# Two first loads on one queue, and four dummy matmuls ahead of the first transpose

## The chip, the cores and the metric

The kernel runs on one core of a Trainium2 chip. A core has five engines that run their own instruction streams and wait for one another through semaphores: TensorE (PE, matmuls and transposes; its weight loads appear as PEld), VectorE (DVE), ScalarE (ACT), GpSimd (POOL) and SyncE (SP). Sixteen DMA engines move data between HBM and the on-chip memory; SP, ACT and POOL issue their transfers. In this kernel POOL's loads run on queue q0 ("software_dynamic"), SP's on q1 and ACT's on q10 (both "hardware_dynamic"); q8 carries instructions.

The metric is the device time of one execution in microseconds (us), here the median of 4 executions: 333.9 us, from 333.14 to 334.2.

## The reference, cut to what matters

Attention with a causal window of 64 positions, over 8 batches and 8 heads of 576 positions with 64 elements each, then a gated feed-forward block on the 4608 x 512 result:

```python
scores = scale * np.matmul(q, k.transpose(0, 1, 3, 2))
mask = (rel >= 0) & (rel < 64)          # rel = query position - key position
attn = softmax(np.where(mask, scores, -1e9))
x = np.matmul(attn, v)                  # -> [4608, 512]
g = x @ w_gate
out = (g / (1 + np.exp(-g)) * (x @ w_val)) @ w_out
```

Inputs and the output are float32. The kernel computes in bfloat16 with float32 accumulation.

## The kernel before, in words

The 4608 tokens are cut into 36 chunks of 128 tokens for the attention and into 9 chunks of 512 tokens for the feed-forward block. For an attention chunk, q and k are transposed (128x128 transposes on PE against an identity matrix, evicted from PSUM by ACT or DVE; for later chunks transposing DMAs on SP), scores are 64-column matmuls, ACT takes their exponential, DVE masks them, PE multiplies by v (which has a column of ones for the sum), DVE divides, and PE transposes the result into xT. The feed-forward block multiplies xT with 128-column blocks of w_gate and w_val (`F`), ACT and DVE form the gated product (`U` is the DVE half), and the last matmuls multiply by w_out (`O`).

The order of the work at the start is written by hand, as two strings of short words in class `_Kernel`: `LOADS`, then `STEPS`. `build` reads them word by word and calls the method that a word names; each call records operations, and `_Graph.emit` later puts every engine's operations in that order into its own stream, with a semaphore wait only where one depends on another engine or on a DMA. The words that matter here:

- `f:0:own` calls `first_load` (L285; the issue has line L291). Chunk 0 is loaded as float32: k into partitions 0 to 63 of the tile ff, q into partitions 64 to 127, 256 KB each. `own` picks the queue of q; k is always on SP:

```python
for eng, p0, src in (("sp", 0, self.k), ("act" if own else "sp", 64, self.q)):
```

- `init` builds the identity, the mask nmask and the zeroed tile wz on DVE (columns 0 to 127 of wz first, at L255; columns 128 to 511 at L271).
- `kq:n`, `v:n`, `w:a:b` issue the loads of chunks and weights on POOL, which casts to bfloat16.
- `warm:65` (L348) puts 65 matmuls of 64 columns on wz at the head of PE's stream. `B:0` (L403) are two matmuls of 512 columns that write the mask into the score banks of chunk 0.
- `ca:0:0` and `cd:0:1` cast the two halves of ff to the bfloat16 tile cc, on ACT (L300) and DVE (L302). Each half holds partitions of both q and k, so both casts need both loads.
- `T:0:1` and `T:0:0` are the first transposes, four a word (L310), each after its half of cc. `ea`, `ed` evict them into kT and qT.
- `W:n` calls `fill` (L359): n matmuls of 512 columns on wz, whose result nobody reads. It looks up the PSUM bank that was free longest and does not reserve it.
- Then chunks 1 to 3: `TQ`, `TK` transposes and `qa`, `kd` evictions, `S` scores (L423), `A0`, `A1` products with v (L473), `M` masks (L439), `N` divisions (L492, L495), `X` transposes (L570), `xa`, `xd` evictions, and from `F:0:7` on the first feed-forward matmuls (L604).

Of the kernel before, what the change touches and what calls it, by code (L numbers as in the profile page):

```python
# [7 lines left out]
B, H, S, D = 8, 8, 576, 64  # L8
DM, DFF = H * D, 1536
T = B * S  # L10
# [139 lines left out]
class _Kernel:  # L150
# [9 lines left out]
    LAST = NFC  # L160
    NI = 1
    LOADS = """
    f:0:1 init kq:1 kq:2 v:0 kq:3 v:1 v:2 v:3 w:7:9 kq:5 kq:4 w:3:4 w:6:7 w:4:5 v:5 w:1:2 v:4 w:9:10 w:2:3 v:6
    w:5:6 v:7 kq:6 w:0:1 kq:7 w:10:12
    """
    STEPS = """
    warm:65 ld:8 wo:0:6 B:0 ca:0:0 cd:0:1 T:0:1 T:0:0 ea:0:1 ed:0:0 TQ:1 qa:1 W:1 S:0 TK:1 ld:9 kd:1 W:1 TQ:2
    qa:2 S:1 B:2 TK:2 kd:2 A0:0 A1:0 M:1 S:2 TQ:3 N:0 B:3 TK:3 qa:3 kd:3 W:1 X:0 A0:1 xa:0 S:3 A1:1 ld:10 A0:2
    N:1 A1:2 ld:11 W:1 A0:3 N:2 A1:3 X:1 xa:1 N:3 W:1 X:2 xa:2 W:3 X:3 F:0:7:0:384 xd:3 U F:0:8 U TK:5 TQ:5
    ka:5 TQ:4 F:0:7:384:512 TK:4 ld:12 qa:4 qd:5 ka:4 U W:2 F:0:3 U S:4 S:5 F:0:6 M:4 F:0:4 M:5 U F:0:1 U U  # L170
    A0:4 A0:5 A1:4 ld:13 wo:6:12 A1:5 F:0:9 N:4 N:5 X:4 F:0:2 U xa:4 X:5 U F:0:5 xd:5 F:1:1:0:128 U TQ:6
    F:1:2:0:256 U TK:6 ld:14 qa:6 F:1:3:0:256 U F:0:0 kd:6 U U S:6 TK:7 TQ:7 F:1:0:0:256 kd:7 F:0:10 M:6 U
    qa:7 U A0:6 S:7 A1:6 ld:15 TQ:8 TK:8 N:6 F:0:11 M:7 ka:8 qd:8 X:6 A0:7 xa:6 U S:8 A1:7 ld:16 F:1:4:0:384
    N:7 F:1:5:0:384 U X:7 U TQ:9 xa:7 F:1:6:0:384 M:8 qa:9 TK:9 U F:1:7 kd:9 TD:10 U A0:8 S:9 A1:8 ld:17 F:1:8
# [610 lines left out]
```

## Time and profile before

| | |
|---|---|
| median of 4 executions | 333.9 us |
| the profiled execution's own time | 334.17 us |
| its span, first to last instruction | 332.4 us |
| PE busy | 325.3 us (98%), 3557 matmuls and 3557 weight loads |
| DVE, ACT, POOL busy | 216.9, 137.4, 115.8 us |
| L310 on cc, the first transposes, start | 6.99 us |
| L604, the first feed-forward matmul, start | 19.31 us |
| L359, dummy matmuls of 512 columns | 10, median 379 ns, longest 631 ns |
| first loads, issue to landing | k on SP 5.7 us, q on ACT 4.1 us |

The profile is of one execution, and its span leaves out what lies before the first and after the last instruction. [...] matmuls that follow one another overlap; what a stream of them costs is read from the distance of their starts. "PEclk" is the clock that TensorE was granted, as a share of its full speed. In a table by windows, each row is a stretch of the span, with every engine's busy time and its number of instructions.

### The profile page before, as it was taken

The numbers are of one execution on the slowest core, as the hardware profiler recorded it, in microseconds if no ns is written. First come the engines' busy times: TensorE is split into PE (matmuls) and PEld (weight loads), VectorE is DVE, ScalarE is ACT, GpSimd is POOL, SyncE is SP. The second block draws the span as 40 slices with busy tenths as digits, with TensorE's granted clock in tenths as the row PEclk, the third lists the DMA queues.
The fourth block names the chain that finished last, engine by engine and source line by source line (L and its number), as shares of the span: only waits on it lengthen the run. The fifth ranks groups of instructions, "written<-read, shape, count | busy, mean of one in ns | idle before, by whom it ended". The sixth has DMA issues, their size and how long they took to land.

```text
span 332.4 us, 8407 instructions
## 1 busy us (share of the span) xinstructions
PE 325.3 (98%) x3557; PEld 166.6 (50%) x3557; DVE 216.9 (65%) x454; ACT 137.4 (41%) x249; POOL 115.8 (35%) x144
## 2 busy tenths in 40 slices
PE   6989999999999999999999999999999999999997
PEld 5654656564454545454545454545454544444444
DVE  6468989994448767676767676767666666555520
ACT  3745456562234525252525243434342522233222
POOL 8999999964008606060706060100000000000000
PEclk9799999999999999999999999999999999999999
DMA  9999999999999999999998989442414111100012
GB/s 132 166 169 172 163 179 156 178 152 150 214 181 114 125 177 76 178 69 187 64 192 61 194 56 182 70 126 34 129 33 127 27 70 28 69 34 32 32 58 103
DMA packets 168837, 38.70 MB, mean 116 GB/s; under 512 B 159328, under 2 KB 164320, under 8 KB 168800
## 3 DMA queue, kind: packets, MB, share of 16 engines
q0 software_dynamic: 122560, 18.62, 81.1%
q1 hardware_dynamic: 45568, 19.21, 28.0%
q8 instruction: 28, 0.46, 0.6%
q10 hardware_dynamic: 672, 0.33, 0.4%
q14 instruction: 9, 0.07, 0.1%
HBM read 37.75 MB, written 9.44 MB: 142 GB/s over the span
## 4 chain that ended last, share of the span: by engine, by line
PE 94%; DVE 2%; DMA 2%; issue 0%; ACT 0%; DVEq 0%
PE ps L604 56%; PE ps L637 28%; PE ps L423 3%; PE ps L536 2%; PE ps L310 2%; DMA ff<-in_k_dram 2%; DVE xb L495 1%; PE ps L473 1%; PE ps L667 1%; PE ps L570 1%; PE ps L403 0%; DVE rc L492 0%; PE ps L359 0%; DVE kT L302 0%; DVE pt L439 0%
## 5 line engine op out<-in xcount | busy, mean ns | idle before, releaser
L613 DVE SCALAR_TENSOR_TENSOR uu<-sig,ps 128x512 bf16<-128x512 bf16 (+3 forms) x116 | 75.3, 649 | 67.4 <-ACT sig L610 67.2
L604 PE MATMUL ps<-xT,Wv 128*128 128x512 bf16 (+3 forms) x464 | 112.3, 364 | 0.6 <-issue 0.6
L604 PE MATMUL ps<-xT,Wg 128*128 128x512 bf16 (+3 forms) x464 | 112.3, 364 | 0.2 <-DVE uu L613 0.2
L610 ACT ACTIVATE sig<-ps 128x512 bf16<-128x512 f32 (+3 forms) x116 | 65.8, 569 | 88.7 <-PE ps L604 88.6
L637 PE MATMUL ps<-Wo,hT 128*128 128x512 bf16 x420 | 97.8, 379 | 0.0
L615 DVE SCALAR_TENSOR_TENSOR hT<-uu,ps 128x512 bf16<-128x512 bf16 (+3 forms) x116 | 75.4, 650 | 4.4 <-PE ps L604 0.5
L373 POOL DMA_DIRECT2D va<-in_v_dram x40 | 40.2, 1031 | 92.1 <-PE ps L536 87.5
L604 PEld LDWEIGHTS ps<-xT,Wv 128*128 128x128 bf16 x464 | 44.6, 98 | 49.9 <-issue 1.0
L604 PEld LDWEIGHTS ps<-xT,Wg 128*128 128x128 bf16 x464 | 43.8, 98 | 46.3 <-DVE xb L495 0.4
L637 PEld LDWEIGHTS ps<-Wo,hT 128*128 128x128 bf16 x420 | 39.9, 98 | 46.6
L433 ACT ACTIVATE pt<-ps 128x512 bf16<-128x512 f32 x72 | 37.7, 600 | 26.7 <-PE ps L423 26.7
L649 ACT ACTIVATE ost<-ps 128x512 f32<-128x512 f32 x35 | 20.9, 597 | 66.1 <-PE ps L637 66.0
L283 POOL DMA_DIRECT2D qn<-in_q_dram x39 | 39.9, 1042 | 3.3 <-issue 2.5
L283 POOL DMA_DIRECT2D kn<-in_k_dram x39 | 40.1, 1048 | 0.0
L439 DVE TENSOR_TENSOR pt<-pt,mask 128x512 bf16<-128x512 bf16 x66 | 24.3, 419 | 0.3
L558 DVE TENSOR_TENSOR xb<-ps,rp 128x448 bf16<-128x448 f32 (+1 forms) x36 | 18.5, 513 | 1.2
L555 DVE RECIPROCAL rp<-ps 128x7 f32<-128x7 f32 (+1 forms) x36 | 6.7, 187 | 15.5 <-PE ps L536 15.5
L423 PE MATMUL ps<-qT,kT 64*64 64x64 bf16 (+1 forms) x864 | 15.9, 205 | 0.5 <-DVE qT L302 0.4
L423 PEld LDWEIGHTS ps<-qT,kT 64*64 64x64 bf16 x864 | 12.4, 109 | 7.1 <-DVE hT L615 4.2
L536 PE MATMUL ps<-va,pt 64*64 64x65 bf16 x728 | 11.5, 193 | 0.1
L495 DVE TENSOR_TENSOR xb<-ps,rc 128x256 bf16<-128x256 f32 x24 | 10.2, 425 | 0.8
L379 POOL DMA_DIRECT2D Wg<-in_moe_w_gate_dram x10 | 9.8, 976 | 0.0
(51 smaller groups left out, 109.7 us busy)
## 6 DMA issues: line engine op xcount, KB each, us to landing
out_dram<-ost SPq DMA_DIRECT2D x35, 256.0 KB, 2.5
va<-in_v_dram POOLq DMA_DIRECT2D x32, 128.0 KB, 6.3
qn<-in_q_dram POOLq DMA_DIRECT2D x31, 128.0 KB, 6.8
kn<-in_k_dram POOLq DMA_DIRECT2D x31, 128.0 KB, 7.2
Wo<-in_moe_w_out_dram POOLq DMA_DIRECT2D x2, 768.0 KB, 11.6
Wg<-in_moe_w_gate_dram POOLq DMA_DIRECT2D x8, 128.0 KB, 5.2
Wv<-in_moe_w_val_dram POOLq DMA_DIRECT2D x8, 128.0 KB, 5.2
Wg<-in_moe_w_gate_dram POOLq DMA_DIRECT2D x2, 256.0 KB, 5.5
```

The source lines that it names most:

```text
L283: self.g.op("pool", lambda e, d=d, a=a: e.dma_start(d, a), writes=ks, dma=True)
L373: g.op("pool", lambda e, d=d, a=a: e.dma_start(d, a), writes=ks, dma=True)
L423: r = e.matmul(sv[h][o:o + 64, c, q0:q1], self.kT[ps, c, kk:kk + 64], qT[ps, c, q0:q1], start=not biased, stop=not biased or c == 3 and kk ...
L433: g.op("act", lambda e, po=po, si=si: e.activation(po, si, ACTF.Exp, scale=SCALE), reads=[bk], writes=[pk])
L439: "dve", lambda e: e.tensor_tensor(po, po, m, ALU.mult), reads=[pk, "mask"], writes=[pk]))
L558: g.op("dve", lambda e, xo=xo, rb=rb, a=a: e.tensor_tensor(xo, a[:, :, 0:64], rb, ALU.mult), reads=[bk] + rk, writes=wk)
L604: r = e.matmul(bank[:, 0:n], W[:, kk, f * 128:f * 128 + 128], xT[:, kk, t0:t1], start=(kk == 0), stop=(kk == NK - 1))
L610: g.op("act", lambda e: e.activation(sig[:, 0:n], G[:, 0:n], ACTF.Tanh, scale=0.5), reads=[gk], writes=[("sig", i)])
L613: g.op("dve", lambda e: e.scalar_tensor_tensor(uu[:, 0:n], sig[:, 0:n], 1.0, G[:, 0:n], ALU.add, ALU.mult), reads=[("sig", i), gk], writes ...
L615: g.op("dve", lambda e: e.scalar_tensor_tensor(hT[:, f, t0:t1], uu[:, 0:n], 0.5, V[:, 0:n], ALU.mult, ALU.mult), reads=[("uu", i), vk], wr ...
L637: r = e.matmul(OB[:, :], hT[:, f, 128 * u:128 * u + 128], self.Wo[:, f, :], start=(f == 0), stop=(f == NF - 1))
L649: g.op("act", lambda e: e.activation(ost[:, :], OB[:, :], ACTF.Copy), reads=[ok], writes=[("ost", io)])
```

## The change

Two words in the strings change. `f:0:1` becomes `f:0:0`, so that q of chunk 0 is issued on SP, directly behind k, and no longer on ACT. `W:4` is inserted between `cd:0:1` and `T:0:1`: four dummy matmuls of 512 columns on wz, ahead of the first transpose in PE's stream. All other words stay as they are and in their order; the lines of `STEPS` are wrapped anew.

```diff
     LOADS = """
-    f:0:1 init kq:1 kq:2 v:0 kq:3 v:1 v:2 v:3 w:7:9 kq:5 kq:4 w:3:4 w:6:7 w:4:5 v:5 w:1:2 v:4 w:9:10 w:2:3 v:6
+    f:0:0 init kq:1 kq:2 v:0 kq:3 v:1 v:2 v:3 w:7:9 kq:5 kq:4 w:3:4 w:6:7 w:4:5 v:5 w:1:2 v:4 w:9:10 w:2:3 v:6
...
     STEPS = """
-    warm:65 ld:8 wo:0:6 B:0 ca:0:0 cd:0:1 T:0:1 T:0:0 ea:0:1 ed:0:0 TQ:1 qa:1 W:1 S:0 TK:1 ld:9 kd:1 W:1 TQ:2
+    warm:65 ld:8 wo:0:6 B:0 ca:0:0 cd:0:1 W:4 T:0:1 T:0:0 ea:0:1 ed:0:0 TQ:1 qa:1 W:1 S:0 TK:1 ld:9 kd:1 W:1
...
```

More of the change, by code (lines that the diff above doesn't have):

```diff
@@ L166 @@
     STEPS = """
-    warm:65 ld:8 wo:0:6 B:0 ca:0:0 cd:0:1 T:0:1 T:0:0 ea:0:1 ed:0:0 TQ:1 qa:1 W:1 S:0 TK:1 ld:9 kd:1 W:1 TQ:2
[L168 to L171, printed above, removed]
+    warm:65 ld:8 wo:0:6 B:0 ca:0:0 cd:0:1 W:4 T:0:1 T:0:0 ea:0:1 ed:0:0 TQ:1 qa:1 W:1 S:0 TK:1 ld:9 kd:1 W:1
+    TQ:2 qa:2 S:1 B:2 TK:2 kd:2 A0:0 A1:0 M:1 S:2 TQ:3 N:0 B:3 TK:3 qa:3 kd:3 W:1 X:0 A0:1 xa:0 S:3 A1:1 ld:10
+    A0:2 N:1 A1:2 ld:11 W:1 A0:3 N:2 A1:3 X:1 xa:1 N:3 W:1 X:2 xa:2 W:3 X:3 F:0:7:0:384 xd:3 U F:0:8 U TK:5
+    TQ:5 ka:5 TQ:4 F:0:7:384:512 TK:4 ld:12 qa:4 qd:5 ka:4 U W:2 F:0:3 U S:4 S:5 F:0:6 M:4 F:0:4 M:5 U F:0:1 U
+    U A0:4 A0:5 A1:4 ld:13 wo:6:12 A1:5 F:0:9 N:4 N:5 X:4 F:0:2 U xa:4 X:5 U F:0:5 xd:5 F:1:1:0:128 U TQ:6
     F:1:2:0:256 U TK:6 ld:14 qa:6 F:1:3:0:256 U F:0:0 kd:6 U U S:6 TK:7 TQ:7 F:1:0:0:256 kd:7 F:0:10 M:6 U
```

## The prediction, on record before the result

> **What bounds the kernel now.** First the page's header, its slices and its chain:
>
> ```profile
> span 332.4 us, 8407 instructions
> PE   6989999999999999999999999999999999999997
> PEclk9799999999999999999999999999999999999999
> PE 94%; DVE 2%; DMA 2%; issue 0%; ACT 0%; DVEq 0%
> ```
>
> PE bounds it from the third slice on (16.6 us); only the first two slices (8.3 us each) have gaps, and the second alone has a reduced clock. Both edits lie there. Whatever delays PE before about 21 us is paid in full, because PE then works to the end without a gap that I found.
>
> Next the chain of waits in order of time, its first and its odd pieces:
>
> ```profile
> 0.73 5.67 DMA ff<-in_k_dram
> ...
> 6.50 0.44 DVE cc L302
> ...
> 6.99 0.63 PE ps L310 x8
> ...
> 10.85 0.97 PE ps L403 x2
> ...
> 20.13 0.64 issue
> ```
>
> The first load sets the start; from 8.9 to 12.3 us the chain runs through slow PE work; at 20.13 PE stands 0.64 us for nothing that a semaphore shows.
>
> Then windows, cut at the edges of the clock record (full speed from 5.465, half from 8.878, full from 12.292 on; each piece is 3.413 us). Columns: stretch, length, then PE, PEld, DVE, ACT, POOL busy with counts, PEclk, DMA share, GB/s.
>
> ```profile
> 5.46:8.88 3.41, 1.54 (x39) 1.11 (x39) 1.68 (x4) 1.78 (x4) 3.41 (x5) 1.00 2.42 154
> 8.88:12.29 3.41, 3.41 (x47) 2.12 (x48) 0.43 (x2) 2.77 (x5) 3.41 (x5) 0.50 2.41 157
> 15.71:19.12 3.41, 2.91 (x62) 1.48 (x63) 3.11 (x12) 2.05 (x4) 3.41 (x6) 1.00 2.33 159
> 19.12:22.53 3.41, 2.77 (x18) 1.41 (x19) 1.53 (x3) 0.53 (x2) 3.41 (x6) 1.00 1.87 175
> ```
>
> After a window in which PE was busy 45% (1.54 of 3.41) the clock was halved for one window; after windows of 85% and 81% it was kept. The gap is the wait for the first load, PE idle from 5.52 to 6.99.
>
> Last, the first loads and their packets (DMA view, windows 0:3.13 and 3.13:4.12):
>
> ```profile
> ff<-in_k_dram SPq DMA_DIRECT2D x1, 256.0 KB, 5.7
> ff<-in_q_dram ACTq DMA_DIRECT2D x1, 256.0 KB, 4.1
> q10 hardware_dynamic: 284, 0.15, 18.2%
> q1 hardware_dynamic: 333, 0.17, 69.0%
> ```
>
> Both are issued at 0.73 and 0.74, yet until 3.13 only q10 (ACT's q) moves anything.
>
> [...]
>
> **Part 1, q behind k on SP.** It removes one ACT issue (0.71 us) and adds a second SP issue (0.74 us), so q is issued at about 1.47 instead of 0.74. ACT's table load may move from 1.49 to about 0.8; ACT then waits for data until 6.49, so nothing comes of it. SP has nothing else before 53 us, and POOL's loads keep their place. What counts is when the second transfer lands. From issue to first packet ACT's took 1.51 us (0.74 to 2.25); from 1.47 that gives 2.98. Packets of q1 began at 3.14[...]. [...] behind k on one queue it has the same place. So k lands near 4.83 and q near 6.41, the roles exchanged: cost 0. Bounds: -0.3 us (if two issues at once held each other up) to +0.74 us (issue time in full).
>
> **Part 2, four matmuls.** They follow the mask matmuls, whose second starts at 4.89 and at half clock takes 0.43 of columns, so 5.33. At full clock 512 columns cost 0.216 (starts 18.218, 18.433, 18.649), at half 0.427: they end between 6.4 and 7.04, against 6.99 for the first transpose. wz is complete at 4.62. Cost 0 to 0.05 us, hidden under the load; without that cover it would be 0.87. The bank that they write is given to `T:0:1` next: same engine, no wait.
>
> **The clock.** The window's busy time rises from 1.54 by about 0.9 (5.52 to 6.42), to 2.44, 71%. The limit is somewhere between 45% and 81%. I take the clock as kept; the other end gives nothing.
>
> **What that releases**, step by step, at full clock from 8.88 on. `TK:1` is evicted at 9.57 (before 9.89); scores of chunk 1 run at 9.61, the two mask matmuls (0.43 for 0.83) to 10.31, `TK:2` to 10.70 (before 12.25). ACT is busy with exponentials until 10.03, so `qa:2` gains only 0.29 and the exponentials of chunk 1 end at 11.71 instead of 12.01. DVE's queue then sets the pace: masks 11.26 to 12.16 (before to 13.38), the division `N:0` (1.18) to 13.26 (before 14.48). So 1.22 us is gained of 1.6 to 1.7 us of PE time. The rest of the start, mostly DVE divisions, moves with it: loads of chunks 1 to 3 land by 14.31, v of chunk 3 is needed after 15, and weights 7 to 9 land at 16.94 against a first use near 18.1.
>
> **What takes part of it back.** What PE has done up to 20.13 (windows), and its next weight load (timeline):
>
> ```profile
> 0.00:20.13 20.13, 16.55 (x347) 11.10 (x347) 12.31 (x43) 10.40 (x19) 19.09 (x28) 0.92 1.82 151
> 20.76 0.11 PEld L604 LDWEIGHTS ps<-xT,Wv 128*128 128x128 bf16 x2 [1.02 <-issue]
> ```
>
> That is 694 instructions[...]. Wv had landed at 16.94; an instruction packet starts at 18.58 and takes 0.95. I read the 0.64 us as the wait for that block. [...] Four matmuls are 8 instructions, with one wait 9, so the edge moves ahead of `F:0:7`'s first four matmuls and the last transpose of `X:3`, which before ran during the fetch (0.65 + 0.06 = 0.71 us). [...] Wv's matmul starts at 20.20 instead of 20.77. Net gain 0.57. Bounds: 1.22 if the stall isn't of this kind or doesn't grow, below zero if the fetch isn't earlier.
>
> **The sum** against the profiled execution's own time: 334.17 + 0 - 1.22 + 0.65 = **333.6 us** (span 331.8). That execution is 0.27 above the median of 333.9, so against the median it is -0.1%. I take 0.3%, 1.0 us, as what a measurement can tell from no change.
>
> **Rivals.**
> - *The gain comes whole.* If the 0.64 us is no block edge, the time is 334.17 - 1.22 = 332.95. For: no view names the cause. Against: [...] the packet at 18.58.
> - *q late, clock kept.* q lands 0.74 later, 333.6 + 0.74 = 334.3. For: the issue is serial. Against: the packets.
> - *q late, clock lost.* The busy time of the window loses what q is late: 2.44 - 0.74 = 1.70, 50%, near the 45% that failed. Then 334.17 + 0.74 + 0.7 (the moved edge) = 335.6. It decides from about 0.4 us of lateness.
> - *The clock falls later* (the other side). [...] the window to 19.12 holds about 2.2 us of work, 65%, less than any that was kept. Half clock from 19.12 falls on 512-column work: up to 3.41 / 2 = 1.7 us, 333.6 + 1.7 = 335.3. For: 65% lies between the window that failed and those that passed. Against: 71% in the first window is hardly more, and I take that as passed. It decides if the limit is above 65%; a limit above 71% would leave the first drop in place as well.
>
> **Chances.** Likeliest 0.50; gain whole 0.14; q late alone 0.09; q late and clock lost 0.10; clock falls later or never rises 0.17. The last two, 0.27, are slower by over 0.3% (above 334.9), with 0.02 of the likeliest's spread: 0.29. Faster (below 332.9) are half of the whole gain and the low end of the likeliest: 0.14. The rest, 0.57, is the same. [...] executions differ, and before's spread of 1.06 us is about the price of one drop. The range for 8 in 10 is 332.8 to 335.4: from the whole gain up to the later fall, leaving out the worst of q late.
>
> **What would show it.** q on q1 landing near 6.4, the casts at 6.5: part 1 right; casts past 6.9: wrong. Four L359 matmuls from 5.33, first transpose at 7.0. PEclk full from 5.5 on, L359 never at 631 ns, `X:0` at 13.3: the clock kept. PE's standstill ahead of or at the first L604 matmul instead of before the Wv ones, and longer than 0.64: the block edge; gone or unmoved: I am wrong there. A half clock after 19 us: the last rival. If casts, clock and standstill are as said and the end doesn't move, then a later wait that I missed sets it.

## The result and the profile after

The change makes the kernel slower: 334.82 us (median of 34 executions, 333.36 to 336.7) against 333.43 us for the kernel before in the same comparison (55 executions, 332.21 to 334.95). The ratio is 1.0046, with a 95% interval of 1.0036 to 1.0057; by the prediction's bound of 0.3% that is slower, not the same. (The 333.9 us given ahead of the prediction for the kernel before was the median of 4 executions.)

The one profiled execution of the changed kernel doesn't look like it. It took 333.4 us, at the fast edge of its kernel, while the profiled execution of the kernel before, 334.17 us, was at the slow edge of its own. Two profiles set side by side would make the change a gain of 0.8 us. Much of what follows is about that trap.

The page of the changed kernel, its header and slices:

```profile
span 331.6 us, 8414 instructions
PE   7979999999999999999999999999999999999997
PEclk9999999999999999999999999999999999999999
```

The reduced clock of the second slice is gone. The chain of waits in order of time (start, length, what), its odd pieces:

```profile
0.74 0.75 SPq L291
1.54 4.84 DMA ff<-in_q_dram
6.41 0.50 DVE cc L302
6.96 0.63 PE ps L310 x8
...
10.16 0.54 PE ps L403 x2
...
18.25 1.55 issue
19.80 3.20 PE ps L604 x16
```

The first load is now q, issued at 1.54 behind k. The mask matmuls of chunk 2 take 0.54 us where they took 0.97. PE reaches the end of the transposes 1.2 us earlier than before (18.25 for 19.48), and then stands for 1.55 us, now ahead of the first feed-forward matmuls; before it was 0.64 us, with the first four of these matmuls already done. The Wv matmuls start at 20.45 instead of 20.77. The same trace by windows, cut at the clock's edges (columns as in the prediction: stretch, length, busy time and count of PE, PEld, DVE, ACT, POOL, then PEclk):

```profile
4.27:7.68 3.41, 2.29 (x27) 1.33 (x24) 2.03 (x6) 0.92 (x3) 3.41 (x5) 1.00 2.03 180
17.92:21.33 3.41, 1.86 (x14) 1.05 (x15) 0.58 (x2) 0.49 (x1) 3.41 (x6) 1.00 2.09 164
```

The window that holds the wait for the first load is now busy 67%, and the clock is kept (1.00 in both rows). The window with the standstill is busy 55%, lower than the 65% that the prediction feared, and here it was still kept. In other executions it was not, as the last experiment shows.

A mean clock is recorded for each execution. One window of half clock makes it 0.995, by an estimate from the profile before (half of 3.41 us, of 332.4 us, is 0.005); that profile, with one such window, has 0.995. The mean clock splits the executions, and medians of the two groups say more than the profiles do:

| | full clock | one window at half clock |
|---|---|---|
| before (66 executions beside the first experiments) | 333.09 us | 333.63 us, 35% of them |
| changed (35 executions, the profiled one included) | 334.39 us | 335.93 us, 13 of 35 |

So the changed kernel is 1.3 us slower even where no clock falls, and a fall costs it 1.54 us instead of 0.54.

### The profile page after: what moved, and what is told of

It reads as the page before. It is cut to its first block, busy times and chain, and to the rows that moved or that the text cites. A ratio compares the mean times of both kernels' runs of the same rounds, so it can differ in the third digit from the quotient of the medians.

```text
span 331.6 us, 8414 instructions
## 1 busy us (share of the span) xinstructions
PE 324.1 (98%) x3561; PEld 166.1 (50%) x3561; DVE 216.9 (65%) x454; ACT 137.2 (41%) x249; POOL 115.8 (35%) x144
## 3 DMA queue, kind: packets, MB, share of 16 engines
q1 hardware_dynamic: 46096, 19.48, 28.7%
## 4 chain that ended last, share of the span: by engine, by line
PE 94%; DVE 2%; DMA 1%; issue 1%; ACT 0%; SPq 0%
PE ps L604 56%; PE ps L637 28%; PE ps L423 3%; PE ps L536 2%; PE ps L310 2%; DMA ff<-in_q_dram 1%; PE ps L473 1%; DVE xb L495 1%; PE ps L667 1%; PE ps L570 1%; DVE kT L302 0%; DVE rc L492 0%; SPq L291 0%; DVE pt L439 0%; ACT sig L610 0%
## 5 line engine op out<-in xcount | busy, mean ns | idle before, releaser
L637 PE MATMUL ps<-Wo,hT 128*128 128x512 bf16 x420 | 97.8, 379 | 0.0
L637 PEld LDWEIGHTS ps<-Wo,hT 128*128 128x128 bf16 x420 | 39.9, 98 | 46.6
```

What stands on the lines that cost most here:

```text
L637: r = e.matmul(OB[:, :], hT[:, f, 128 * u:128 * u + 128], self.Wo[:, f, :], start=(f == 0), stop=(f == NF - 1))
```

## The experiments

After the result the theory ("block edge" below) was: PE stands because it waits for the next packet of instructions on q8, and the eight instructions of the four matmuls (four matmuls, four weight loads) put this standstill ahead of the first four Wg matmuls. So the loss is that moved edge, plus a clock that falls behind the longer standstill; the queue of q costs nothing. Where in PE's stream that edge lies was the author's estimate, set against the standstill in the profile before. The rival: the loss comes from q behind k on one queue. The ratios below are to the kernel before, measured beside each kernel. The diffs show a changed line up to the place of the change; the rest of the line stays as it is.

**One part alone.** The four matmuls without the queue (`f:0:1` kept):

```diff
-    warm:65 ld:8 wo:0:6 B:0 ca:0:0 cd:0:1 T:0:1 T:0:0
+    warm:65 ld:8 wo:0:6 B:0 ca:0:0 cd:0:1 W:4 T:0:1 T:0:0
```

> Only the four dummy matmuls; q of chunk 0 stays on ACT. Theory (block edge): [...] standstill before the first Wg matmul of 1.2 to 1.6 us instead of 0.64 before the Wv ones; time as the whole change, ratio to before 1.003 to 1.006. Rival (queue): the loss comes from q behind k on SP; then this run is at before or below it, 0.997 to 1.000.

Measured: 1.0021 (1.0006 to 1.0035), median 333.67. With full clock it is 333.66, that is 0.57 above the kernel before with full clock. The chain of its profile:

```profile
18.22 1.56 issue
19.78 2.34 PE ps L604 x12
```

The standstill is where the theory puts it, but the loss is less than half of the whole change. Three of 22 executions had a fallen clock; they took 335.58 to 336.38.

The queue without the matmuls:

```diff
-    f:0:1 init kq:1 kq:2
+    f:0:0 init kq:1 kq:2
```

> Only q of chunk 0 on SP behind k. Theory (block edge): PE's instructions are as before and q lands near 6.4, as k did before, so 0.999 to 1.001 and a standstill of about 0.6 us before the Wv matmuls. Rival (queue): all of the loss is here, 1.004 to 1.005, with the casts past 6.9 us in typical executions.

Measured: 1.0029 (1.0017 to 1.0042), median 334.09. The theory had 0.999 to 1.001 and is wrong here; the rival had all of the loss here, and is wrong too. Both parts cost. In its profile the standstill is before the Wv matmuls again, 0.91 us; q landed at 6.53. Of its executions 73% had a fallen clock, against 35% for the kernel before. That fits the prediction's third rival, in which PE waits longer for a later first load, but doesn't show it: the transposes start at 7.04 in this profile, and at 6.99 in the one before. The profile of this run has a full clock, so where the clock fell in the others isn't seen.

**The edge, moved without its cause.** The whole change, with four warming matmuls fewer, so that PE's count ahead of the feed-forward matmuls is as before:

```diff
-    warm:65 ld:8 wo:0:6 B:0 ca:0:0 cd:0:1 W:4 T:0:1
+    warm:61 ld:8 wo:0:6 B:0 ca:0:0 cd:0:1 W:4 T:0:1
```

> The whole change, with 61 in place of 65 matmuls of 64 columns at the head, so that PE has as many instructions ahead of the first L604 matmul as the kernel before. Theory (block edge): the standstill is back before the Wv matmuls; time at or below before, 0.997 to 1.000, the rest being what the full clock saves. Rival (queue) or rival (the four matmuls' own work): still 1.004 to 1.005.

Measured: 1.0008 (0.9998 to 1.0018), median 333.52. Its profile, an execution at the slow end (335.04), shows where the standstill went:

```profile
19.53 0.65 PE ps L604 x4
20.18 1.19 issue
21.36 1.69 PE ps L604 x8
```

The four Wg matmuls run ahead of it, as before the change. Most of the loss is gone, though queue and dummy matmuls are still there; what is left is q's landing (7.11 in this execution), less what the kept clock saves.

And the kernel before, with four warming matmuls more and nothing else:

```diff
-    warm:65 ld:8 wo:0:6 B:0 ca:0:0 cd:0:1 T:0:1
+    warm:69 ld:8 wo:0:6 B:0 ca:0:0 cd:0:1 T:0:1
```

> The kernel before with 69 in place of 65 matmuls of 64 columns at the head: 8 more PE instructions, no dummy matmul of 512 columns, queues as before. They end near 4.7 us, well before the first load lands. Theory (block edge): standstill ahead of the Wg matmuls, 1.003 to 1.007. Rivals (queue; the four matmuls' own work): 0.999 to 1.001.

Measured: 1.0029 (1.0011 to 1.0048), median 334.11. Eight PE instructions that end well before anything waits for them cost 0.8 us:

```profile
19.16 0.40 PE ps L570 x4
19.56 0.74 issue
20.30 1.91 PE ps L604 x10
```

The standstill has moved ahead of the Wg matmuls, with queues and dummy matmuls as before.

**The edge moved back.** The dummy matmuls with q on ACT, and 61 warming matmuls:

```diff
-    warm:65 ld:8 wo:0:6 B:0 ca:0:0 cd:0:1 T:0:1
+    warm:61 ld:8 wo:0:6 B:0 ca:0:0 cd:0:1 W:4 T:0:1
```

> The four dummy matmuls, q on ACT, 61 matmuls of 64 columns at the head: PE's count as before, queues as before. Theory: edge where it was before and a clock that seldom falls, so 333.0 to 333.3, ratio 0.998 to 1.000; beside the run with the four matmuls alone it gives the price of the moved edge, about 0.6 us. Rival (the four matmuls cost by their own work): as that run, 1.002.

Measured: 0.9993 (0.9981 to 1.0004), median 332.78 against 332.94; no fallen clock in 13 executions. It is the best of all, and not shown to be faster than the kernel before. Beside the run with the four matmuls alone (1.0021) it puts the moved edge at 0.3%, with intervals that nearly touch; the price expected for it was 0.6 us, 0.2%. With full clock alone, each beside the kernel before with full clock, it is 0.54 us (0.57 less 0.03).

The same with 53, so that the edge falls behind 16 more instructions:

```diff
-    warm:65 ld:8 wo:0:6 B:0 ca:0:0 cd:0:1 T:0:1
+    warm:53 ld:8 wo:0:6 B:0 ca:0:0 cd:0:1 W:4 T:0:1
```

> The four dummy matmuls, q on ACT, and 53 in place of 65 matmuls of 64 columns at the head: 16 PE instructions fewer than before ahead of the feed-forward matmuls. Theory (block edge): the edge falls behind the Wv matmuls and the next Wg ones, some 2.2 us of work, more than the standstill that is left, so the standstill is gone or under 0.3 us and the time is 332.0 to 332.4, ratio 0.996 to 0.998. Rival (no edge, the standstill belongs to the first feed-forward matmuls or to the time at which they start): standstill of 0.6 to 1.6 us as before, ratio 0.999 to 1.002.

Measured: 1.0000 (0.9989 to 1.0011), median 332.93. The standstill is gone, as the theory says, and the time is not better. PE's waits from 17 to 75 us in this kernel, and then in the kernel before from 24 to 75 us (engine and line, what it waited for, us in total, times, longest):

```profile
PE ps L637 <- DVE uu L613: 1.0, 1, 1.0
PE ps L604 <- issue: 0.6, 4, 0.2
```

```profile
PE ps L604 <- DVE uu L613: 0.2, 1, 0.2
```

What PE gains at 20 us it waits for at 73 us in this kernel, where the first output matmul (L637) needs a product that DVE has not formed yet. From there to the end all these kernels take the same, 257.8 to 258.3 us in the traces. That matmul starts at 72.87 us here, and at 72.74 in the kernel with 61 warming matmuls, which has the standstill. So an early gain can be lost again, as here.

The kernel before with 57 warming matmuls, and nothing else:

```diff
-    warm:65 ld:8 wo:0:6 B:0 ca:0:0 cd:0:1 T:0:1
+    warm:57 ld:8 wo:0:6 B:0 ca:0:0 cd:0:1 T:0:1
```

> The kernel before with 57 in place of 65 matmuls of 64 columns: 16 PE instructions fewer, nothing else. Theory (block edge): the standstill before the Wv matmuls goes, 0.997 to 0.999. Rival (the number of warming matmuls sets the time by the clock): fewer warming matmuls, so slower, 1.001 to 1.004.

Measured: 1.0017 (1.0004 to 1.0031), median 333.59. The standstill is gone here as well, and PE waits 1.48 us for DVE before the first output matmul, at 73.38. Neither side had the time right: the theory expected a gain. That PE's wait for DVE takes the gain away is seen; why the time is above that of the kernel before is open.

**A standstill made longer.** The whole change with 69 warming matmuls, which should move the edge 8 instructions further ahead:

```diff
-    warm:65 ld:8 wo:0:6 B:0 ca:0:0 cd:0:1 W:4 T:0:1
+    warm:69 ld:8 wo:0:6 B:0 ca:0:0 cd:0:1 W:4 T:0:1
```

> The whole change with 69 in place of 65 matmuls of 64 columns: the edge moves 8 instructions further ahead, before the three dummy matmuls that cover the last division. Theory (block edge, and a clock that falls when PE stands too long): standstill from about 17 us on for 2 us or more, PEclk halved for one piece after about 18 to 21 us in most executions, 335.5 to 336.5, ratio 1.006 to 1.009. Rival (edge without the clock): 334.8 to 335.3. Rival (neither): as the whole change, 334.8.

Measured: 1.0073 (1.0052 to 1.0094), median 335.66; three of four executions with a fallen clock. The chain of its profile:

```profile
18.16 2.29 issue
20.45 0.38 PE ps L570 x4
20.83 0.67 PE ps L604 x4
...
22.80 2.74 PE ps L604 x7
```

The last transposes wait too, one group earlier than in the change: four transposes and their four weight loads are the 8 instructions. The expectation had put the place three dummy matmuls further ahead, which is 6 instructions too many. The clock record has half speed from 21.54 to 24.95, and the mean clock is 0.995.

**Why q lands late.** First the other queue: k and q both on ACT.

```diff
-        for eng, p0, src in (("sp", 0, self.k), ("act" if own else "sp", 64, self.q)):
+        for eng, p0, src in (("act", 0, self.k), ("act", 64, self.q)):
```

> The whole change, but k and q of chunk 0 both on ACT's queue in place of SP's. Theory (the second transfer of one queue starts late, whichever queue it is): q's packets begin after k's have ended, near 3.9 to 4.2 us, and q lands at 6.4 to 7.1. Rival (SP's queue is the slow one): packets from 3.1 to 3.2 on, landing at 5.6 to 6.2.

Measured: q landed at 6.84, one execution, 334.07 us. So the late landing isn't SP's alone: q as second on ACT's queue lands late too. Over all profiles of this study but the next one, q behind k lands at 6.39 to 7.11, mean 6.66 of ten; on two queues the later of the two lands at 5.59 to 6.41, mean 5.98 of six, the kernel before being the latest of them.

Then POOL's first load held until k has landed (a wait on k's semaphore at the head of POOL's loads; `self.first` is the issue of k, which a second changed line keeps):

```diff
-                self.g.op("pool", ..., writes=ks, dma=True)
+                self.g.op("pool", ..., writes=ks, dma=True, after=[self.first] if (n, nm) == (1, "qn") else [])
```

> The whole change, but POOL's first load waits until k has landed, so that nothing shares the DMA engines with q before some 6 us; everything after the first loads is later by about 3.5 us, and so is the end. Theory (late start, then half the engines): q's packets still begin near 3.9 us but end by 5.2, and q lands by 5.7. Rival (the late landing is the sharing alone): packets begin at 3.1 to 3.2, landing by 5.0. Rival (sharing plays no part): landing at 6.4 to 7.1 as in the change.

Measured: q landed at 5.69; one execution, 335.43 us, since all later loads are late. The DMA view of the stretch 3.13 to 4.2 us (queue, packets, MB, share of 16 engines), for the kernel before, the change, and this one:

```profile
q1 hardware_dynamic: 370, 0.19, 72.3%
q10 hardware_dynamic: 244, 0.12, 36.8%
q0 software_dynamic: 18, 0.00, 3.4%
```

```profile
q0 software_dynamic: 453, 0.06, 84.4%
q1 hardware_dynamic: 276, 0.13, 44.4%
```

```profile
q1 hardware_dynamic: 613, 0.31, 119.3%
```

With k and q on two queues, the DMA engines move 614 packets of both in this stretch, and 18 of POOL's q0. With both on one queue, q0 gets 453 packets in between, and from 3.7 to 4.2 us q's data nearly halts (34 packets of q1, 274 of q0). With POOL held back, q1 moves 613 packets in the stretch, 231 of them from 3.7 to 4.2. So q's packets need not start late at all: POOL's queue goes in between, and has the larger part afterwards too (1671 packets of q0 and 499 of q1 from 4.2 to 6.6 us in the change). POOL issues its first load at 1.24 us in the change and at 1.25 in the kernel before, yet between 3.13 and 3.7 us q0 has 179 packets in the change and none in the kernel before. Why q0 begins earlier where one queue is in use beside it stays open. Neither the theory's late start nor its rival's landing by 5.0 was met; the landing by 5.7 was.

**Where the clock falls in the change itself.** Five more executions of the changed kernel unaltered, each with its profile, since the first profile had a full clock.

> The whole change once more, for a second execution's profile: 13 of 35 executions had a mean clock of 0.995. Theory: where the clock falls, it falls for 3.41 us after 19 to 23 us, behind the standstill, and the first feed-forward matmuls run at half speed. Rival: it falls at 8 to 10 us, as it did before. With a full clock the run only shows the standstill of 1.2 to 1.6 us and q's landing at 6.4 to 7.1.

Measured: 333.87 us, full clock, standstill 1.56 us, q at 6.78.

> As the look before it: a fall of the clock between 19 and 23 us and 335.5 to 336.7, or a full clock and 333.4 to 335.2; the rival puts the fall before 12 us.

Measured: 335.95 us, mean clock 0.995. The others were expected alike: 333.83, 334.07 and 333.68 us, full clock, standstills of 1.6 to 1.8 us, q at 6.55 to 6.57. The execution of 335.95 us by windows at the clock's edges, and its chain:

```profile
17.30:20.71 3.41, 1.25 (x9) 0.44 (x7) 1.09 (x4) 0.60 (x1) 3.41 (x6) 1.00 2.19 163
20.71:24.13 3.42, 3.20 (x10) 1.52 (x10) 1.11 (x2) 0.49 (x1) 3.42 (x5) 0.50 1.86 176
```

```profile
18.45 2.11 issue
20.56 2.63 PE ps L604 x8
```

The standstill was 2.11 us here and filled one window: PE was busy 37%, and the clock was halved from 20.71 to 24.13, over matmuls of 384 and 512 columns on the path. That is the fall at 19 to 23 us which the theory expected, not the one at 8 to 10 us of the kernel before. It is the only execution of the changed kernel with a fallen clock that has a profile.

**What ends the standstill.** Queue q8 is the one that the page names "instruction". In the kernel before (packets, MB, share of 16 engines):

```profile
q8 instruction: 28, 0.46, 0.6%
```

That is 16 KiB a packet, and in each profile one of them falls near the standstill (us from the start of the span):

| profile | packet starts | PE goes on | from one to the other |
|---|---|---|---|
| before | 18.58 | 20.77 | 2.19 |
| changed | 17.55 | 19.80 | 2.24 |
| changed, the execution of 335.95 us | 18.05 | 20.56 | 2.51 |
| changed, 61 warming matmuls | 19.06 | 21.36 | 2.30 |
| changed, 69 warming matmuls | 18.19 | 20.45 | 2.26 |
| changed, POOL held | 19.42 | 21.77 | 2.35 |

In all 15 profiles with a standstill PE goes on 2.19 to 2.51 us after that packet's start, although the time at which it goes on moves by 2.3 us (19.51 to 21.77) and the place in PE's stream from the transposes to the Wv matmuls. So the standstill ends at a steady distance from an instruction packet; that the packet is the cause is the author's reading of these times, and no view names it.

## Why the prediction was wrong, step by step

It forecast 333.6 us and no difference; the changed kernel takes 334.82, 1.4 us more than before. The step that failed is the cost of 0 for q behind k; the gain put on the clock was mis-sized too, and a later fall of the clock stood outside the sum, as a rival. The terms, at full clock unless said:

- *Part 1, "behind k on one queue it has the same place. ... cost 0": wrong*, and the step that failed most. Measured: 0.73 us, from the four matmuls alone (333.66) to the whole change (334.39), of which 0.1 us is a difference of the kernel before between these two sets of runs. Two other pairs give 0.77 us (the queue alone, 334.09 for 333.32) and 0.5 us (with 61 warming matmuls, ratios 1.0008 for 0.9993). q lands 0.68 us later on average than the later load of two queues. The issue time was rightly seen to be no limit (with POOL held back q, issued behind k as well, landed at 5.69); it was overlooked that POOL's queue moves its packets between those of k and q (453 of q0 from 3.13 to 4.2 us). The 6.41 us forecast for q was nearly met in the change's first profile (6.39) and missed by 0.25 on average (6.66); the rest of the 0.68 is that the profile before, with k at 6.41, was the latest of six and was taken as typical.
- *Part 2, the four matmuls hidden under the load: right.* The timeline has them from 4.82 to 5.85, sooner than the 5.33 expected because the full clock is on record from 4.27 in this execution (from 5.465 in the profile before), and the first transpose at 6.96. The four records of 0.38 us each take 1.03 together: they overlap.
- *The clock kept: right* in all six profiles of the change, after the first load. But it was credited with 1.22 us against an execution that had lost it. Within the profiles that size came true: PE reaches the end of the transposes 1.23 us earlier. But only 35% of the executions of the kernel before lose the clock, and those are 0.54 us slower, so the term is worth about 0.2 us, to the mean (0.35 x 0.54) and to the median (333.32 for all, 333.09 with full clock). The prediction said that executions differ and that its profile was above the median, and still made the sum against that profile. That its 333.6 us is where the four matmuls alone do end with full clock (333.66) is in part luck: the start of 334.17 was 0.54 above the median of the executions with a fallen clock (333.63), and the gain of 1.22 was 0.68 too large.
- *What takes part of it back: right as to the place and nearly in size.* Expected 0.71 us for the four matmuls that no longer run during the standstill, measured 0.57. In the profile PE went on at 19.80 us, and Wv's matmul started at 20.45, not at 20.20. That the standstill follows the count of PE's instructions is shown by the seven kernels in which that count was altered or put back; that a packet of instructions ends it rests on the times alone (2.19 to 2.51 us from packet to PE). How long ahead the packet is asked for, on which the 20.20 rested, was the author's estimate and is not shown.
- *"PE then works to the end without a gap that I found": wrong.* PE waited 0.22 us for DVE at 73.77 us in the kernel before, and 1.0 and 1.5 us in the two kernels without a standstill. The line of slices, too, was misread: it is the third slice that stands at 8, and it holds the standstill at 20.13.
- *The rival of a later fall: it came, but not for its reason*, and at 0.17 it was ranked too low. 13 of 35 executions lose the clock, for 1.54 us where 1.7 was worked out. That all of them lose it after 19 us is not shown: it is inferred from the price and from the one fallen execution that has a profile. The rival put the window at 65% busy and needed a limit above that. Windows of 52 and 55% kept the clock; it fell where the standstill was 2.11 us long and lay whole in one window, which left 37%.

So the 334.82 us measured lie 1.2 us above the 333.6 forecast, about 0.7 of it for q (0.1 of that the difference between sets of runs) and 0.4 for the later falls (334.39 with full clock, 334.82 for all). These terms are differences of the same medians, so that they add up is no test of them. The term for q is backed by the other two pairs of runs; the term for the falls only by the split by clock.

## What to carry to other kernels

Profile more than one execution before a fraction of a percent is argued from a trace: here the clock's fall sat in a third of them, and the sum was made against one of these. Count an inserted instruction also by where it pushes the ones behind it; eight instructions on PE that nothing waits for cost 0.8 us here. Two first loads that must both land before anything starts were better on two queues here, by 0.5 to 0.77 us, where a third queue moved its packets beside them (from 3.13 to 4.2 us 453 in the change, 18 in the kernel before).

## What the runs showed that was not expected

- A standstill of PE that no semaphore explains moves with the number of PE instructions ahead of it and can be placed: before the Wv matmuls (0.64 us), before the Wg ones (1.55), before the last transposes (2.29), or nowhere. It ends 2.19 to 2.51 us after the start of an instruction packet.
- Between the clock's edges PE was busy 52% of 3.41 us in the second profile of the change (16.64 to 20.06 us), and the clock was kept; it was 48% in the kernel before with 69 warming matmuls (5.31 to 8.72 us), and the clock was halved, as after 45% and 37%. These shares give no limit: with 57 warming matmuls the clock was kept after 48% (4.81 to 8.22 us), and with k and q both on ACT after 44% (4.57 to 7.98 us, where the trace has three of the four dummy matmuls; with the fourth it would be about 50%, by an estimate from the other three). The mean clock of both profiles is 1.0.
- POOL's q0 has packets from 3.08 to 3.37 us on in the ten profiles with k and q on one queue and POOL free, and from 3.97 to 4.26 us on in the six with two, though POOL issues its first load at 1.24 to 1.25 us in all of them. That order, not the issue time (0.61 to 0.75 us), goes with the later landing.
